# Masking the transposed probabilities instead of the right-hand side, and sending the last zero fill as one plain transfer

## The chip, the cores and the metric

The kernel runs on one core of a Trainium2 chip. The metric is the device time of one execution in microseconds (us); less is better. Engines are named as in the profile: PE (matrix multiplication), DVE (vector), ACT (scalar), POOL (GpSimd) and SP (sync). SP, ACT and POOL issue DMAs; 16 DMA engines carry them out.

## The reference, cut to what matters

One decode step of a transformer block, and the gradients of everything in it. The output is a row of 448 numbers; the caches have 8 heads of 32768 keys of 256 numbers, and only the last 4096 keys are attended to.

```
W = 4096
q = layernorm(x) @ wq;  k = k_cache[:, :, Sk - W:, :];  v = v_cache[:, :, Sk - W:, :]
p = softmax(q k / 16);  o = p v;  h = x + o @ wo
h2 = h + (gate(layernorm(h)) * up(layernorm(h))) @ w_down
outputs: h2, and d(x), d(k_cache), d(v_cache), d(wq), d(wo), d(w_gate), d(w_up), d(w_down)
```

All numbers are bf16. The gradients of the two caches have the full size of the caches, 134 MB each: zero for the first 28672 keys of each head, and for the last 4096 a sum of two outer products, since two query heads share a key head: dV = p dO and dK = dS q, one row per key.

## The kernel before, in words

**Zero fills.** The zero part of the cache gradients is written by DMA from a block of zeros in SBUF, `zeros`, 128 partitions by 8192 numbers (2 MB a transfer). The list `fills` has 103 such blocks (lines 119 to 126). POOL issues them: the first 55 at the start (lines 135 and 136), the next 47 from line 434 on, behind the second feed-forward block, and the last one, `fills[-1]`, at the end of the program in four pieces (lines 660 to 667). The pieces take their rows from 5, 3, 8 and 4 partitions: 10 rows of 576 B, 24 of 16384 B, 72 of 16304 B and 32 of 16384 B. Five more fills, `late_jobs`, four of 4 MB and one of 2 MB, are issued by SP (line 671).

**First pass** (lines 331 to 342): a loop over the 8 key heads computes scores and softmax, and moments of K and V. **Middle** (lines 363 to 493): the output projection, the feed-forward part and its backward pass.

**Second pass** (lines 605 to 655): a loop over the 8 key heads again, with its position `it` and its head `g`. For each head it

1. transposes V in blocks and multiplies (function `dots`, lines 245 to 262), which gives dP;
2. builds `pds`, 128 by 128: for each of 32 key tiles (4 quarters q of 8 tiles l) four columns, the probabilities and dS of two query heads, and transposes it on PE into `r_ps` (line 624), which DVE copies to SBUF as `rT` (line 626). Row 32 q + 4 l + i of `rT` has the numbers of key tile (q, l) and column i;
3. spreads dO and q of the head over 128 rows as `R_sb`, 128 by 512 (lines 627 to 633);
4. multiplies `R_sb` by the mask `tl_f`, 128 by 8, which is 1 where the row belongs to tile l: `RB_`, 128 by 8 by 512 (line 635), in one of two buffers `Rbig`;
5. for each l and q multiplies 32 rows of `rT` with 32 rows of `RB_[:, l]` on PE (line 643), which gives dV and dK of one key tile. Since the mask has zeros in 28 of the 32 rows, one tile comes out. DVE and ACT copy the results to SBUF (lines 647 to 651), in place of V and into one of two buffers at `dK_off`;
6. stores both, 2 MB each, by SP (line 653), and runs the jobs that `plan` gives to this position: the weight gradients (lines 541 to 599), which SP stores too.

Order of the work: a tile scheduler derives it from priorities and data dependences, so an edit may move instructions of any engine. SP's DMAs share eight semaphores in turn, and so do POOL's, so that each has at most eight DMAs in flight. In the program of SP the last entries are: the stores of the head at `it` 5, those of the feed-forward weights, the stores of `it` 6, one 4 MB late fill, the stores of `it` 7, and the three last late fills.

Of the kernel before, what the change touches and what calls it, by code (L numbers as in the profile page):

```python
# [7 lines left out]
bf16 = mybir.dt.bfloat16  # L8
f32 = mybir.dt.float32
AX = mybir.AxisListType.X  # L10
ALU = mybir.AluOpType
# [15 lines left out]
ZW = 8192  # L27
# [6 lines left out]
def kernel(  # L34
# [19 lines left out]
    def ar(off, n):  # L54
        return arena[:, off:off + n]
# [29 lines left out]
    VT_slot = [ar(RB + (40 + 2 * i) * KB, 2 * KB).rearrange("p (e t k) -> p e t k", t=4, e=2) for i in range(3)]  # L85
    Zr = ar(RB + 46 * KB, KB).rearrange("p (w k i) -> p w k i", w=4, k=32)
    rows2 = ar(RB + 47 * KB, 2 * KB)[0:16].bitcast(f32)
    Rbig = [ar(RB + 8 * KB * i, 8 * KB).rearrange("p (l n) -> p l n", l=8) for i in range(2)]
    dK_off = [RB + 16 * KB, A_off[2]]
    wst = [ar(A_off[3 + i], 16 * KB) for i in range(2)]  # L90
    dg_bc = ar(A_off[5], 2 * F).rearrange("p (i f) -> p i f", i=2)
# [36 lines left out]
    def send_fills(n0, n1, halves=False):  # L128
        for reg in fills[n0:n1]:
            if halves:  # L130
                ZQ.dma_start(out=reg.rearrange("p (k f) -> p k f", k=2), in_=zeros[:, 0:ZW // 2].unsqueeze(1).to_broadcast([128, 2, ZW // 2]))
            else:
                ZQ.dma_start(out=reg, in_=zeros)  # L133
# [229 lines left out]
    with tc.tile_pool(name="ps_mid", bufs=3, space=bass.MemoryType.PSUM) as ps_mid, \  # L363
# [34 lines left out]
        for n in range(len(BLOCKS)):  # L398
            f0, nb, w, wgu, wd = block_views(n)
            b0 = f0 // 128  # L400
            cs = slice(b0, b0 + nb)
            for b in range(nb):
                nc.vector.tensor_tensor_reduce(out=dgb[:, 0:D], in0=wd[:, b, :], in1=dh2_bc[:], scale=1.0, scalar=0.0,
                                               op0=ALU.mult, op1=ALU.add, accum_out=d_hh[:, b0 + b:b0 + b + 1])
            gu_ps = ps_mid.tile([128, 2, 5], f32, tag="mid", name="gu_ps")
            for i in range(2):
                for b in range(nb):
                    for k in range(4):
                        kp = DQ if k == 3 else 128
                        nc.tensor.matmul(gu_ps[:, i, b:b + 1], lhsT=wgu[0:kp, k, i, b::nb], rhs=X2_b[0:kp, k:k + 1], start=(k == 0), stop=(k == 3))  # L410
            nc.vector.tensor_copy(out=gu_f[:, :, cs], in_=gu_ps[:, :, 0:nb])
            for i in range(2):
                nc.vector.tensor_tensor(out=dgu_f[:, i, cs], in0=d_hh[:, cs], in1=gu_f[:, 1 - i, cs], op=ALU.mult)
            nc.vector.tensor_tensor(out=hh_f[:, cs], in0=gu_f[:, 0, cs], in1=gu_f[:, 1, cs], op=ALU.mult)
            nc.vector.tensor_copy(out=hh_bf[:, cs], in_=hh_f[:, cs])
            for i in range(2):
                nc.vector.tensor_tensor(out=diag[:, 0:w].rearrange("p (m b) -> p m b", b=nb), in0=ident_f[:].unsqueeze(2).to_broadcast([128, 128, nb]),
                                        in1=dgu_f[:, i, cs].unsqueeze(1).to_broadcast([128, 128, nb]), op=ALU.mult)
                for m in range(2):
                    bc_ps = ps_mid.tile([128, 320], f32, tag="mid", name="bc_ps")  # L420
                    nc.tensor.matmul(bc_ps[:, 0:w // 2], lhsT=ones_bf[:], rhs=diag[:, m * w // 2:(m + 1) * w // 2], start=True, stop=True)
                    nc.scalar.copy(out=dgb[:, w * i + m * w // 2:w * i + (m + 1) * w // 2], in_=bc_ps[:, 0:w // 2])
            for b in range(nb):
                nc.tensor.matmul(ffn_ps[:], lhsT=hh_bf[:, b0 + b:b0 + b + 1], rhs=wd[:, b, :], start=(b0 + b == 0), stop=(b0 + b == NF - 1))
            for c in range(4):
                kp = DQ if c == 3 else 128
                wc = wgu[0:kp, c].rearrange("p i f -> p (i f)")
                nc.vector.tensor_tensor_reduce(out=wc, in0=wc, in1=dgb[0:kp, 0:2 * w], scale=1.0, scalar=0.0,  # L428
                                               op0=ALU.mult, op1=ALU.add, accum_out=dhn[0:kp, c, n:n + 1])
            if n + 2 < len(BLOCKS):  # L430
                load_block(n + 2)
            if n == 1:
                nc.vector.memset(ar(ZW // 2, ZW // 2), 0.0)
                send_fills(HALF1, len(fills) - 1)

        dcat2 = workm.tile([128, 8], f32)
        nc.vector.reduce_sum(out=dcat2[:, 0:4], in_=dhn[:], axis=AX)
# [57 lines left out]
    with tc.tile_pool(name="work2", bufs=2) as work2, tc.tile_pool(name="lnw", bufs=1) as lnw, \  # L495
# [109 lines left out]
        for it, g in enumerate(order):  # L605
            V_sb = kv_at(V2_off[it])
            fill_vpad(it % 2, doT_bf[:, :, 2 * g:2 * g + 2])

            def evac(q, XT, ps):
                if q % 2:  # L610
                    nc.scalar.copy(out=XT, in_=ps)  # L611
                else:
                    nc.vector.tensor_copy(out=XT, in_=ps)  # L613
            dpT_ps = dots(V_sb, VT_slot, vpad[it % 2], rows2, ps_t, "tmp", evac)

            pds = work2.tile([128, 4, 8, 4], bf16, tag="pds")
            pv = pT_all[:, g].rearrange("p (q l) h -> p q l h", q=4)
            tmp = work2.tile([128, T, 2], f32, tag="tmp2")
            nc.vector.tensor_tensor(out=tmp[:], in0=dpT_ps[:].rearrange("p q l h -> p (q l) h"),
                                    in1=delta_bc[:, 2 * g:2 * g + 2].unsqueeze(1).to_broadcast([128, T, 2]), op=ALU.subtract)  # L620
            nc.vector.tensor_copy(out=pds[:, :, :, 0:2], in_=pv)
            nc.vector.tensor_tensor(out=pds[:, :, :, 2:4], in0=tmp[:].rearrange("p (q l) h -> p q l h", q=4), in1=pv, op=ALU.mult)
            r_ps = ps_t.tile([128, 128], bf16, tag="tmp")
            nc.tensor.transpose(r_ps[:], pds[:].rearrange("p q l i -> p (q l i)"), ident_bf[:])
            rT = work2.tile([128, 128], bf16, tag="rT")
            nc.vector.tensor_copy(out=rT[:], in_=r_ps[:])
            nc.vector.tensor_copy(out=Zr, in_=Z4[:, :, :, g, :].rearrange("p w e i -> p (w e) i").unsqueeze(2).to_broadcast([128, 4, 32, 4]))
            R_ps = ps_t.tile([128, 2, 2, 128], f32, tag="tmp")
            for w in range(2):
                for dh in range(2):  # L630
                    nc.tensor.matmul(R_ps[:, w, dh, :], lhsT=Zr[:, 2 * w + dh].rearrange("p k i -> p (k i)"), rhs=ident_bf[:], start=True, stop=True)
            R_sb = work2.tile([128, 512], bf16, tag="R", bufs=1)
            nc.scalar.copy(out=R_sb[:], in_=R_ps[:].rearrange("p w e n -> p (w e n)"))  # L633
            RB_ = Rbig[it % 2]
            nc.vector.tensor_tensor(out=RB_, in0=R_sb[:].unsqueeze(1).to_broadcast([128, 8, 512]),  # L635
                                    in1=tl_f[:].unsqueeze(2).to_broadcast([128, 8, 512]), op=ALU.mult)
            stV, stK = V_sb, kv_at(dK_off[it % 2])
            for l in range(8):
                for qp in range(2):
                    d_ps = ps_d.tile([128, 2, 2, Dh], f32, tag="d")  # L640
                    for qi in range(2):
                        q = 2 * qp + qi
                        nc.tensor.matmul(d_ps[:, qi].rearrange("p w d -> p (w d)"), lhsT=rT[32 * q:32 * (q + 1), :], rhs=RB_[32 * q:32 * (q + 1), l, :],  # L643
                                         start=True, stop=True)
                    t = 4 * l + 2 * qp
                    if qp:
                        nc.scalar.copy(out=stV[:, t:t + 2, :], in_=d_ps[:, :, 0, :])  # L647
                        nc.scalar.copy(out=stK[:, t:t + 2, :], in_=d_ps[:, :, 1, :])  # L648
                    else:
                        nc.vector.tensor_copy(out=stV[:, t:t + 2, :], in_=d_ps[:, :, 0, :])  # L650
                        nc.vector.tensor_copy(out=stK[:, t:t + 2, :], in_=d_ps[:, :, 1, :])  # L651
            for o_ap, st_ in ((out_3, stV), (out_2, stK)):
                LD.dma_start(out=o_ap[0, g, Sk - W:, :].rearrange("(p t) d -> p t d", t=T), in_=st_)
            for job in plan[it]:
                job()
            if it == 6:

                nc.vector.memset(ar(ZW, ZW), 0.0)

        flat = fills[-1].rearrange("p f -> (p f)")  # L660
        base = 0
        for p0, k, m, w in ((0, 5, 2, 288), (20, 3, 8, ZW), (64, 8, 9, ZW - 40), (0, 4, 8, ZW)):
            n = k * m * w
            ZQ.dma_start(out=flat[base:base + n].rearrange("(k m f) -> k m f", k=k, m=m),
                         in_=zeros[p0:p0 + 4 * k - 3:4, 0:w].unsqueeze(1).to_broadcast([k, m, w]))
            base += n
        assert base == 128 * ZW
        for o, g, n0, n1, f in late_jobs:
            reg = zero_rows(o, g, n0, n1, f)
            for i in range(reg.shape[0]):  # L670
# [30 lines left out]
```

## Time and profile before

| what | value |
|---|---|
| median of 4 runs | 797.76 us (796.17 to 797.96) |
| profiled execution, its own time | 797.22 us |
| its span, first to last instruction | 795.4 us |
| bytes moved by DMA | 334.77 MB |
| busy: PE, DVE, ACT, POOL | 59%, 55%, 25%, 8% of the span |

Times in the trace count from the start of the span. A group line gives the source line, engine, operation, operands with partitions x elements, the count, the busy time and the mean of one in ns, and the idle time ahead of it with what ended it. A window line gives for each engine the busy time and the number of instructions, then PE's granted clock, the share of the 16 DMA engines that was busy, and the rate.

### The profile page before, as it was taken

What the parts mean: (1) busy time and instruction counts of PE and PEld (TensorE: products, weight loads), DVE (VectorE), ACT (ScalarE), POOL (GpSimd) and SP (SyncE); (2) the same over time, 40 slices, a digit from 0 to 9 for tenths busy, and PEclk for the clock granted to TensorE, in tenths of its full rate; (3) what the DMA queues carried; (4) which work ended last, traced back from release to release, by engine and by line L of the source; (5) the groups of instructions that cost most, each with busy time, mean ns of one, the idle gap of its engine ahead of it and who ended that gap; (6) DMA issues with size and microseconds to landing.
All of it is one profiled execution on the core that took longest, in us unless ns stands there. A gap on an engine that the chain in (4) does not pass through costs nothing.

```text
span 795.4 us, 7324 instructions
## 1 busy us (share of the span) xinstructions
PE 470.7 (59%) x2926; PEld 220.4 (28%) x2926; DVE 436.7 (55%) x629; ACT 196.0 (25%) x309; POOL 63.4 (8%) x115
## 2 busy tenths in 40 slices
PE   0459999999999998251409477673450553722000
PEld 0333434344344433121208334330220210300000
DVE  2116584765846782263690679598653874964000
ACT  0142314134132201010102126362320441534000
POOL 4000000010101111100210001000000000010000
PEclk9989999999999999655558769695565556865555
DMA  9999999999999999999999999999999999999996
GB/s 350 430 429 429 431 429 431 430 428 426 431 423 425 429 418 414 422 422 425 431 429 424 421 430 427 427 428 427 423 424 424 423 425 422 428 419 417 430 438 297
DMA packets 29688, 334.77 MB, mean 421 GB/s; under 512 B 3150, under 2 KB 6230, under 8 KB 8150
## 3 DMA queue, kind: packets, MB, share of 16 engines
q0 software_dynamic: 16832, 216.01, 64.2%
q1 hardware_dynamic: 11382, 116.68, 34.9%
q10 hardware_dynamic: 1440, 1.61, 0.6%
q8 instruction: 23, 0.38, 0.2%
q14 instruction: 11, 0.09, 0.0%
HBM read 53.69 MB, written 280.59 MB: 420 GB/s over the span
## 4 chain that ended last, share of the span: by engine, by line
PE 39%; DMA 30%; DVE 15%; ACT 5%; issue 2%; another core or an unknown queue 0%; SPq 0%; DVEq 0%; ACTq 0%
DMA out_dram<-arena 21%; PE M_ps L317 13%; PE ok_ps L320 8%; PE rows_ps L256 6%; PE tr_ps L253 4%; DMA dh_bc<-in_grad_out_dram 4%; ACT arena L270 3%; DMA arena<-in_B_w_down_dram 3%; DVE arena L459 2%; PE dqb_ps L502 2%; DMA arena<-in_B_w_gate_dram 2%; DVE arena L635 2%; DVE arena L428 1%; DVE arena L514 1%; DVE arena L650 1%
## 5 line engine op out<-in xcount | busy, mean ns | idle before, releaser
L312 DVE TENSOR_TENSOR arena<-arena,p_f 128x2048 bf16<-128x2048 bf16 x64 | 145.4, 2286 | 60.5 <-PE M_ps L317 60.4
L317 PE MATMUL M_ps<-arena 128*128 128x512 bf16 x512 | 128.9, 380 | 0.2 <-ACT arena L323 0.2
L643 PE MATMUL d_ps<-arena,rT 32*128 32x512 bf16 x256 | 46.0, 506 | 116.4 <-DVE arena L651 67.4
L253 PE MATMUL tr_ps<-ident_bf,arena 128*128 128x128 bf16 x1024 | 89.4, 237 | 19.1 <-ACT arena L611 11.4
L256 PE MATMUL rows_ps<-arena,vpad 128*16 128x512 bf16 x256 | 87.2, 435 | 21.1 <-DVE arena L613 15.2
L133 POOL DMA_DIRECT2D out_dram<-arena x89 | 47.8, 539 | 528.5 <-DMA out_dram<-arena 494.0
L253 PEld LDWEIGHTS <-arena 128*128 128x128 bf16 x1024 | 66.9, 106 | 70.3 <-issue 61.8
L270 ACT COPY arena<-tr_ps 128x1024 bf16<-128x1024 bf16 x64 | 61.8, 1015 | 64.0 <-PE tr_ps L253 64.0
L647 ACT CAST arena<-d_ps 128x512 bf16<-128x512 f32 x64 | 37.7, 588 | 125.8 <-PE d_ps L643 125.8
L320 PE MATMUL ok_ps<-arena 128*16 128x512 bf16 x256 | 63.8, 381 | 0.9 <-DVE arena L297 0.9
L317 PEld LDWEIGHTS <-arena 128*128 128x128 bf16 x512 | 43.3, 99 | 59.0 <-issue 23.2
L611 ACT COPY arena<-tr_ps 128x1024 bf16<-128x1024 bf16 x32 | 32.6, 1019 | 94.3 <-PE rows_ps L256 34.6
L651 DVE CAST arena<-d_ps 128x512 bf16<-128x512 f32 x64 | 43.4, 678 | 13.6 <-DMA out_dram<-arena 13.6
L643 PEld LDWEIGHTS <-rT 32*128 32x128 bf16 x256 | 11.4, 95 | 142.0 <-issue 93.4
L650 DVE CAST arena<-d_ps 128x512 bf16<-128x512 f32 x64 | 43.7, 683 | 12.6 <-PE d_ps L643 12.0
L648 ACT CAST arena<-d_ps 128x512 bf16<-128x512 f32 x64 | 38.0, 594 | 14.4 <-DMA out_dram<-arena 14.4
L635 DVE TENSOR_TENSOR arena<-R_sb,tl_f 128x4096 bf16<-128x4096 bf16 x8 | 35.3, 4416 | 0.7 <-ACT R_sb L633 0.7
L256 PEld LDWEIGHTS <-vpad 128*16 128x16 bf16 x256 | 19.0, 91 | 58.1 <-issue 50.2
L320 PEld LDWEIGHTS <-arena 128*16 128x16 bf16 x256 | 19.1, 89 | 41.5 <-issue 20.3
L514 DVE CUSTOM_DVE_ANT_0 arena<-arena 128x4096 bf16<-128x4096 bf16 x3 | 13.1, 4420 | 24.5 <-ACT arena L507 24.5
L285 ACT ACTIVATE e_f<-cols_ps,nbias 128x32 f32<-128x32 f32 x16 | 4.5, 285 | 86.8 <-DVE nbias L281 86.8
L258 DVE COPY arena<-rows_ps 16x512 f32<-16x512 f32 x16 | 10.8, 676 | 26.4 <-PE rows_ps L256 26.3
(199 smaller groups left out, 389.1 us busy)
## 6 DMA issues: line engine op xcount, KB each, us to landing
out_dram<-arena POOLq DMA_DIRECT2D x102, 2048.0 KB, 52.3
out_dram<-arena SPq DMA_DIRECT2D x18, 2048.0 KB, 32.8
arena<-in_A_v_cache_dram SPq DMA_DIRECT2D x10, 2048.0 KB, 49.5
arena<-in_A_k_cache_dram SPq DMA_DIRECT2D x8, 2048.0 KB, 29.0
out_dram<-arena SPq DMA_DIRECT2D x4, 4096.0 KB, 43.1
arena<-in_A_wq_dram SPq DMA_DIRECT2D x2, 3072.0 KB, 20.6
arena<-in_A_wo_dram SPq DMA_DIRECT2D x2, 1792.0 KB, 14.2
out_dram<-arena SPq DMA_DIRECT2D x2, 1792.0 KB, 15.1
```

What stands on the lines that cost most here:

```text
L133: ZQ.dma_start(out=reg, in_=zeros)
L253: nc.tensor.transpose(tr_ps[:, dh, i, :], X_sb[:, 4 * q + i, dh * 128:(dh + 1) * 128], ident_bf[:])
L256: nc.tensor.matmul(rows_ps[:], lhsT=pad[:, dh, 16 * q:16 * q + 16], rhs=XT[:, dh].rearrange("p t k -> p (t k)"), start=(q == 0 and dh == 0 ...
L270: sT_ps = dots(kv_at(K_off[g]), KT_slot, vpad[g % 2], rows1, ps_c, "cols", lambda q, XT, ps: nc.scalar.copy(out=XT, in_=ps))
L312: nc.vector.tensor_tensor(out=pK, in0=K_sb[:, 4 * c:4 * c + 4, :].unsqueeze(2).to_broadcast([128, 4, 2, Dh]), in1=p_f[:, c::8, :].unsqueez ...
L317: nc.tensor.matmul(M_ps[:, vh, :], lhsT=V_sb[:, t, vh * 128:(vh + 1) * 128], rhs=pK[:, i, :, :].rearrange("p h d -> p (h d)"), start=(t == ...
L320: nc.tensor.matmul(ok_ps[:].rearrange("p k d -> p (k d)"), lhsT=ppad[g % 2][:, 8 * (t % 4) + t // 4, :], rhs=both(g, t), start=(g == 0 and ...
L635: nc.vector.tensor_tensor(out=RB_, in0=R_sb[:].unsqueeze(1).to_broadcast([128, 8, 512]), in1=tl_f[:].unsqueeze(2).to_broadcast([128, 8, 51 ...
L643: nc.tensor.matmul(d_ps[:, qi].rearrange("p w d -> p (w d)"), lhsT=rT[32 * q:32 * (q + 1), :], rhs=RB_[32 * q:32 * (q + 1), l, :], start=T ...
L648: nc.scalar.copy(out=stK[:, t:t + 2, :], in_=d_ps[:, :, 1, :])
L650: nc.vector.tensor_copy(out=stV[:, t:t + 2, :], in_=d_ps[:, :, 0, :])
L651: nc.vector.tensor_copy(out=stK[:, t:t + 2, :], in_=d_ps[:, :, 1, :])
```

## The change

The mask moves from the right-hand side (4096 columns) to the transposed probabilities (1024 columns): `rT` is not copied out of PSUM but multiplied by the mask on the way, once for each l, and the product on PE takes slice l of it with the unmasked `R_sb`. The buffers `Rbig` go; the two new operands have two buffers each. Independently of this, the last zero fill goes out as the others do, in one transfer of 128 rows behind the 102nd, and the four pieces go.

```diff
-    Rbig = [ar(RB + 8 * KB * i, 8 * KB).rearrange("p (l n) -> p l n", l=8) for i in range(2)]
+    rT_slot = [ar(RB + 2 * KB * i, 2 * KB).rearrange("p (l n) -> p l n", l=8) for i in range(2)]
+    R_slot = [ar(RB + (4 + i) * KB, KB) for i in range(2)]
...
-                send_fills(HALF1, len(fills) - 1)
+                send_fills(HALF1, len(fills))
...
-            rT = work2.tile([128, 128], bf16, tag="rT")
-            nc.vector.tensor_copy(out=rT[:], in_=r_ps[:])
+            rTm = rT_slot[it % 2]
+            nc.vector.tensor_tensor(out=rTm, in0=r_ps[:].unsqueeze(1).to_broadcast([128, 8, 128]),
+                                    in1=tl_f[:].unsqueeze(2).to_broadcast([128, 8, 128]), op=ALU.mult)
...
-            R_sb = work2.tile([128, 512], bf16, tag="R", bufs=1)
-            nc.scalar.copy(out=R_sb[:], in_=R_ps[:].rearrange("p w e n -> p (w e n)"))
-            RB_ = Rbig[it % 2]
-            nc.vector.tensor_tensor(out=RB_, in0=R_sb[:].unsqueeze(1).to_broadcast([128, 8, 512]),
-                                    in1=tl_f[:].unsqueeze(2).to_broadcast([128, 8, 512]), op=ALU.mult)
+            R_sb = R_slot[it % 2]
+            nc.scalar.copy(out=R_sb, in_=R_ps[:].rearrange("p w e n -> p (w e n)"))
...
-                        nc.tensor.matmul(d_ps[:, qi].rearrange("p w d -> p (w d)"), lhsT=rT[32 * q:32 * (q + 1), :], rhs=RB_[32 * q:32 * (q + 1), l, :],
+                        nc.tensor.matmul(d_ps[:, qi].rearrange("p w d -> p (w d)"), lhsT=rTm[32 * q:32 * (q + 1), l, :], rhs=R_sb[32 * q:32 * (q + 1), :],
...
-        flat = fills[-1].rearrange("p f -> (p f)")
-        base = 0
-        for p0, k, m, w in ((0, 5, 2, 288), (20, 3, 8, ZW), (64, 8, 9, ZW - 40), (0, 4, 8, ZW)):
-            n = k * m * w
-            ZQ.dma_start(out=flat[base:base + n].rearrange("(k m f) -> k m f", k=k, m=m),
-                         in_=zeros[p0:p0 + 4 * k - 3:4, 0:w].unsqueeze(1).to_broadcast([k, m, w]))
-            base += n
-        assert base == 128 * ZW
```

In the order of the instructions, the changed program has one more plain fill on POOL (103, without a wait on DVE), and on SP the 4 MB late fill that stood ahead of the stores of `it` 7 stands behind them; the 896-column store of the feed-forward weights stands between the stores of `it` 6 and `it` 7.

## The prediction

> **What bounds the kernel.** I read the 40 slices first, then the bytes, the windows at the end, SP's DMAs in order of time, and last the groups that the change touches.
>
> ```profile
> DMA  9999999999999999999999999999999999999996
> GB/s 350 430 429 429 431 429 431 430 428 426 431 423 425 429 418 414 422 422 425 431 429 424 421 430 427 427 428 427 423 424 424 423 425 422 428 419 417 430 438 297
> ...
> HBM read 53.69 MB, written 280.59 MB: 420 GB/s over the span
> ```
>
> From the first slice to the last but one the 16 DMA engines are 90% busy or more, at about 425 GB/s; 334.77 MB at that rate are 788 of the 795.4 us of the span. No other engine is over 59%. The chain of waits names PE and DVE for more than half, but only because a DMA queue with work left shows as no wait. So the end is set by the bytes, and by how evenly the 16 engines finish. The second shows in the windows at the end (PE, PEld, DVE, ACT, POOL busy; clock; DMA share; GB/s):
>
> ```profile
> 740.00:760.00 20.00, 0.00 (x0) 0.00 (x0) 0.00 (x0) 0.00 (x0) 0.00 (x0) 0.50 1.01 431
> ...
> 786.00:787.00 1.00, 0.00 (x0) 0.00 (x0) 0.00 (x0) 0.00 (x0) 0.00 (x0) 0.50 1.00 426
> 787.00:788.00 1.00, 0.00 (x0) 0.00 (x0) 0.00 (x0) 0.00 (x0) 0.00 (x0) 0.50 0.77 328
> 788.00:789.00 1.00, 0.00 (x0) 0.00 (x0) 0.00 (x0) 0.00 (x0) 0.00 (x0) 0.50 0.54 229
> 789.00:790.00 1.00, 0.00 (x0) 0.00 (x0) 0.00 (x0) 0.00 (x0) 0.00 (x0) 0.50 0.50 213
> 790.00:791.00 1.00, 0.00 (x0) 0.00 (x0) 0.00 (x0) 0.00 (x0) 0.00 (x0) 0.50 0.34 147
> 791.00:792.00 1.00, 0.00 (x0) 0.00 (x0) 0.00 (x0) 0.00 (x0) 0.00 (x0) 0.50 0.27 115
> 792.00:793.00 1.00, 0.00 (x0) 0.00 (x0) 0.00 (x0) 0.00 (x0) 0.00 (x0) 0.50 0.19 82
> 793.00:794.00 1.00, 0.00 (x0) 0.00 (x0) 0.00 (x0) 0.00 (x0) 0.00 (x0) 0.50 0.08 33
> ```
>
> No compute has run since 740. From 787 to 794 the engines fall out one by one. The shares add up to 2.69, which is 2.69 us of all 16 engines, spread over 7: had all ended together, that would have been some 4 us sooner.
>
> **Who ends when.** The trace keeps start, duration, size and queue of each DMA packet, not its engine. But an engine starts a packet 3 to 4 ns before its last one ends, so that the packets string into 16 chains, back from the end, where the starts lie apart. I did this from the end back to where the four pieces of the last fill run (about 735 to 749 on the packets' own clock, which is some 10.3 us ahead of the span's: the last packet ends at 804.4 on it). Every packet found a place. The chains fall into four kinds by what they hold of the fill: nine rows of 16304 B (8 chains); eight rows of 16384 B alone (3), or with a short row of 1152 B (4); and one chain with the short row only. Their ends:
>
> - 16304 B: 796.9, 797.2, 797.7, 798.0, 798.0, 799.9, 799.9, 800.2
> - 16384 B: 799.6, 800.2, 802.0, 802.9, 803.9, 804.1, 804.4
> - nothing but the short row: 801.6
>
> So the pieces give one engine next to nothing, and eight engines a little more than the other seven; the one that is spared still ends at 801.6, later than the mean of 800.4.
>
> **The change, part by part.**
>
> *The last fill.* It leaves the bytes as they are, and gives each engine eight rows of 16384 B. Rows of this size took 611 ns alone and about 618 while compute ran (means of the packets). The spared engine gains 8 x 0.618 = 4.9 us of work and loses its short row and about 30 packets of 4 B at 9 ns that belong to the pieces (0.3 us): 801.6 + 4.6 = 806.2. The eight lose one row (0.6 us), and everybody about 0.2 us of small packets. The last end moves from 804.4 to 806.2: **+1.8 us**. When the fill is issued doesn't matter: POOL's queue still moved the rows of the plain fills ahead of it when the pieces came, so it takes its turn in the same stream. POOL's wait goes, and nothing was behind it:
>
> ```profile
> POOL out_dram L664 <- DVE arena L651: 35.4, 1, 35.4
> ```
>
> *Rule against row.* The Trainium skill, "DMA: Bandwidth & Descriptors", section "Rules for kernel authors", asks for 128 partitions and at least 1 MiB per DMA, and its section on the anatomy of a DMA gives about 2.0 us fixed for each; by that, one transfer instead of four would save 6 us. The trace says that the fixed part is covered: the pieces take 32 to 35 us to land in a queue at a share of 1.01.
>
> *The mask.* The groups:
>
> ```profile
> L312 DVE TENSOR_TENSOR arena<-arena,p_f 128x2048 bf16<-128x2048 bf16 x64 | 145.4, 2286 | 60.5 <-PE M_ps L317 60.4
> L635 DVE TENSOR_TENSOR arena<-R_sb,tl_f 128x4096 bf16<-128x4096 bf16 x8 | 35.3, 4416 | 0.7 <-ACT R_sb L633 0.7
> L613 DVE COPY arena<-tr_ps 128x1024 bf16<-128x1024 bf16 x32 | 21.6, 680 | 3.0 <-PE tr_ps L253 2.4 <-PE rows_ps L256 0.3
> L626 DVE COPY rT<-r_ps 128x128 bf16<-128x128 bf16 x8 | 1.7, 213 | 0.0
> ```
>
> Eight of 4416 ns and eight copies of 213 go; eight products of 1024 columns out of PSUM come. From 2048 and 4096 columns the slope is 2130 / 2048 = 1.04 ns and the fixed part 156 ns, so 1221 ns for 1024. Bounds: 680 (a copy of that size out of PSUM) and 2286 (the 2048-column product). I take 1221, the same operation. DVE saves 8 x (4416 + 213 - 1221) = 27 us; by the bounds 19 to 32 us. PE's matmuls and weight loads keep count and shape (256 of each). The product waits for what the copy waited for, and holds the one PSUM buffer of its tag 1.0 us longer; the four R matmuls, which need that buffer next, wait for it, 8 us in all, but where they waited the big product came behind them: 33.6 us of PE waiting on line 635 go.
>
> None of the 27 us reaches the end. The second pass waits for its own stores: in the chain, DMA stretches of 15 to 43 us stand between the heads. SP's queue says the same (start, duration):
>
> ```profile
> 703.30 13.36 SPq L653 DMA_DIRECT2D out_dram<-arena  x2
> 716.72 11.36 SPq L671 DMA_DIRECT2D out_dram<-arena  x1
> 731.00 3.95 SPq L653 DMA_DIRECT2D out_dram<-arena  x2
> 736.96 4.75 SPq L671 DMA_DIRECT2D out_dram<-arena  x3
> ```
>
> Everything is issued by 742, and the engines work until 794. DVE time saved turns into waits for stores. Value taken: **0**. Its bounds: less compute beside DMA could make rows faster, 618 ns towards 611, over at most the last 30 us, 0.3 us; the other way, 0.
>
> *SP's order.* The 4 MB late fill moves behind the last stores. These may find SP's and POOL's queues empty; then the engines idle. At 731, 25.1 MB were left (the windows from there on), 14.7 MB of them in transfers issued at 731 or later; so 10.4 MB stood ahead, and 6.2 MB without that fill. At 425 GB/s that is 14.6 us of cover: the last head's compute may be 14 us later than now, and it has less to do. So 0. If the cover is gone, each us more costs one.
>
> **Sum.** 797.22 + 1.8 = 799.0 for an execution like the profiled one. The median of the runs is 0.54 above that execution, and I forecast the median: **799.5 us** (+0.2%).
>
> **Rivals.**
>
> 1. *The spared engine isn't always the slowest.* For it: it ended in the middle of the seven, and ends differ by 5 us among engines with equal bytes. If it comes out 2 us earlier, the 804.4 engine still ends last: 797.2 - 0.2 = 797.0, with the median's distance 797.5, no change.
> 2. *Faster: the ends even out.* Which engine is late may depend on the stream, and the pieces themselves may have made it uneven. If the spread falls to half, the last end comes 2 us sooner, and the median is 795.7; it decides once the engine that takes the 4.9 us is one of those that end before 799. Against it: the spared engine was late even though spared.
> 3. *Slower by more: a hole ahead of the last fills.* It needs the last head 14.6 us later than now. With 3 to 5 us of idle engines beyond the 1.8: 802.5 to 804.5. Against it: DVE has 27 us less to do.
> 4. *The mask pays after all*, if stores that come earlier shorten the stream: 796 at best. Against it: the engines have no gap to fill, and more than 50 us at the end pass without compute.
>
> **Chances.** Forecast 0.62, with its own range 798.5 to 801.5; rival 1 0.18; rivals 2 and 4 together 0.10; rival 3 0.10. A measurement of this kernel can tell about 0.2% from no change, 1.6 us: the border to slower is 799.4, inside the forecast's own range. I put three quarters of it, 0.48, above. So slower 0.48 + 0.10 = 0.58; same 0.14 + 0.18 = 0.32; faster 0.10. The range reaches from rival 1's 797.0 to 801.8, just past the forecast's own upper end.
>
> **What would show it.** Right: a DMA share of 1.0 up to about 787, then a longer tail in which the share falls to one engine (0.06) for the last 2 us; the chain that ended at 801.6 is last; a new DVE group of eight at about 1.2 us; DVE's busy time 27 us less, and DVE's and SP's waits for stores longer. Wrong: no lone engine at the end (rivals 1 and 2), or a share well under 1.0 between 730 and 760 (rival 3). Over 803 or under 796 would say that the engines' lags don't carry from one program to the next.

## The result and the profile after

The changed kernel takes **798.96 us** in the median (798.46 to 800.34, 38 runs); the kernel before, with more runs, 797.30 us (795.14 to 799.01, 56 runs). The ratio is 1.002, with a 95% interval of 1.0015 to 1.0025: slower by 1.66 us. The profiled execution after took 798.80 us, with a span of 797.0 us, 1.6 us more than before.

The page of the kernel after, DMA in 40 slices and in sums:

```profile
DMA  9999999999999999999999999999999999999995
GB/s 350 428 431 430 431 427 429 432 431 423 433 422 426 427 418 414 422 421 425 434 429 421 425 428 429 428 428 423 425 426 425 422 427 421 424 426 420 437 428 257
DMA packets 29352, 334.76 MB, mean 420 GB/s; under 512 B 2819, under 2 KB 5894, under 8 KB 7814
...
HBM read 53.69 MB, written 280.59 MB: 419 GB/s over the span
```

The same bytes move at nearly the same rates, slice by slice; only the last slice is emptier (257 GB/s instead of 297), because the DMA engines end less evenly. There are 336 packets fewer: 331 of them have 4 or 8 B, and the other five are the short rows of the pieces. The windows at the end show the tail (columns as before; the last two are the DMA share and GB/s):

```profile
740.00:760.00 20.00, 0.00 (x0) 0.00 (x0) 0.00 (x0) 0.00 (x0) 0.00 (x0) 0.50 1.02 432
...
789.00:790.00 1.00, 0.00 (x0) 0.00 (x0) 0.00 (x0) 0.00 (x0) 0.00 (x0) 0.50 0.35 147
790.00:791.00 1.00, 0.00 (x0) 0.00 (x0) 0.00 (x0) 0.00 (x0) 0.00 (x0) 0.50 0.12 49
791.00:792.00 1.00, 0.00 (x0) 0.00 (x0) 0.00 (x0) 0.00 (x0) 0.00 (x0) 0.50 0.19 82
792.00:793.00 1.00, 0.00 (x0) 0.00 (x0) 0.00 (x0) 0.00 (x0) 0.00 (x0) 0.50 0.11 49
793.00:794.00 1.00, 0.00 (x0) 0.00 (x0) 0.00 (x0) 0.00 (x0) 0.00 (x0) 0.50 0.08 33
794.00:795.00 1.00, 0.00 (x0) 0.00 (x0) 0.00 (x0) 0.00 (x0) 0.00 (x0) 0.50 0.08 33
```

Before, a third of the engines still worked at 790; after, only an eighth do, and yet the end is later. From 793 on the share is 0.08, about one engine of 16. The chains of packets, strung as in the prediction, say the same: 13 engines end from 797.0 to 800.6, and three behind them at 802.4, 804.3 and 806.2 (on the packets' clock).

The mask's groups, and SP's DMAs in order of time (start, duration):

```profile
L627 DVE TENSOR_TENSOR arena<-r_ps,tl_f 128x1024 bf16<-128x1024 bf16 x8 | 9.7, 1215 | 0.8 <-PE r_ps L625 0.8
```

```profile
705.95 5.68 SPq L652 DMA_DIRECT2D out_dram<-arena  x2
711.69 5.73 SPq L584 DMA_DIRECT2D out_dram<-arena  x1
731.20 1.63 SPq L652 DMA_DIRECT2D out_dram<-arena  x2
734.23 13.00 SPq L662 DMA_DIRECT2D out_dram<-arena  x4
```

DVE is busy for 410.2 us instead of 436.7. Its last stores are issued at 731.2; before, with 26 us more to do, at 731.0. Most of the time saved went into waits for stores that had not landed: those of DVE (all lines together) grew from 57 to 79 us. The longest, before and after (the columns: us in total, times, longest):

```profile
DVE arena L539 <- DMA out_dram<-arena: 22.4, 2, 15.6
```

```profile
DVE arena L540 <- DMA out_dram<-arena: 33.4, 3, 22.4
```

This is a job waiting for its buffer.

### The profile page after: what moved, and what is told of

Same layout as the page of the kernel before. It is cut to its first block, busy times and chain, and to the rows that moved or that the text cites. A ratio compares the mean times of both kernels' runs of the same rounds, so it can differ in the third digit from the quotient of the medians.

```text
span 797.0 us, 7310 instructions
## 1 busy us (share of the span) xinstructions
PE 470.6 (59%) x2926; PEld 220.1 (28%) x2926; DVE 410.2 (51%) x621; ACT 195.9 (25%) x309; POOL 61.1 (8%) x112
## 4 chain that ended last, share of the span: by engine, by line
PE 41%; DMA 27%; DVE 16%; ACT 4%; issue 2%; another core or an unknown queue 2%; SPq 0%; DVEq 0%; ACTq 0%
DMA out_dram<-arena 18%; PE M_ps L318 13%; PE ok_ps L321 8%; PE rows_ps L257 7%; PE tr_ps L254 5%; DMA dh_bc<-in_grad_out_dram 4%; ACT arena L271 3%; DMA arena<-in_B_w_down_dram 3%; DVE arena L460 2%; DVE arena L649 2%; PE dqb_ps L503 2%; DMA arena<-in_B_w_gate_dram 2%; DVE arena L545 2%; DVE arena L650 2%
## 5 line engine op out<-in xcount | busy, mean ns | idle before, releaser
L642 PE MATMUL d_ps<-arena 32*128 32x512 bf16 x256 | 45.1, 506 | 98.6 <-DVE arena L650 84.0
L642 PEld LDWEIGHTS <-arena 32*128 32x128 bf16 x256 | 10.9, 95 | 124.1 <-issue 77.4
L540 DVE TENSOR_SCALAR arena<-arena,xT 128x1792 bf16<-128x1792 bf16 (+1 forms) x9 | 7.7, 881 | 33.4 <-DMA out_dram<-arena 33.4
```

## The experiments

Theory: one DMA engine always has more to do than the others, the four pieces spared it, and the plain fill doesn't. Rival A: the mask, or the new order of SP's stores, made the kernel slower. Rival B: four pieces sent late are good in themselves, whichever engine they spare. The time of the kernel before that stands beside a run was taken on the same chip.

### One part of the change at a time

The mask edit with the four pieces kept:

```diff
-                send_fills(HALF1, len(fills))
+                send_fills(HALF1, len(fills) - 1)
...
+        for p0, k, m, w in ((0, 5, 2, 288), (20, 3, 8, ZW), (64, 8, 9, ZW - 40), (0, 4, 8, ZW)):
```

> The mask edit alone; the last fill stays in its four pieces. Theory (the end is set by the DMA engine that has most to move; the four pieces spare one that is always late): the last packet ends as before, no change against before, ratio 1.000 within 0.0007, 797.0 to 797.8 us, and DVE's busy time 27 us less than before. Rival A (the mask, or the order of SP's stores that it changes, made the kernel slower): ratio 1.002, about 799 us. Rival B (the pieces help only through their shape or their late issue): ratio 1.000 too.

Measured: 797.34 us against 797.37, ratio 0.9996 (0.9987 to 1.0004); DVE is busy for 410.4 us. The last packet ends at 804.3 on the packets' clock (804.4 before). In this program SP's late fill stands behind the last stores as it does after, and the kernel is no slower. Rival A is out.

The plain fill with the mask on 4096 columns:

```diff
-                send_fills(HALF1, len(fills) - 1)
+                send_fills(HALF1, len(fills))
...
-        for p0, k, m, w in ((0, 5, 2, 288), (20, 3, 8, ZW), (64, 8, 9, ZW - 40), (0, 4, 8, ZW)):
```

> The last fill alone goes plain; the mask stays on the 4096 columns. Theory: ratio to before 1.002, about 799.0 us, and a lone DMA engine (share 0.06 to 0.08) in the last 2 us. Rival A: ratio 1.000. Rival B: ratio 1.002 too.

Measured: 798.91 us, ratio 1.0019 (1.0011 to 1.0028). The last packet ends at 806.4, the one before it at 804.5. The windows 793 to 795 have the lone engine again:

```profile
793.00:794.00 1.00, 0.00 (x0) 0.00 (x0) 0.00 (x0) 0.00 (x0) 0.00 (x0) 0.50 0.12 49
794.00:795.00 1.00, 0.00 (x0) 0.00 (x0) 0.00 (x0) 0.00 (x0) 0.00 (x0) 0.50 0.08 33
```

The fill alone is the whole of the change's effect.

### How much cover DVE has

```diff
             nc.vector.tensor_tensor(out=RB_, in0=R_sb[:].unsqueeze(1).to_broadcast([128, 8, 512]),
                                     in1=tl_f[:].unsqueeze(2).to_broadcast([128, 8, 512]), op=ALU.mult)
+            nc.vector.tensor_tensor(out=RB_, in0=R_sb[:].unsqueeze(1).to_broadcast([128, 8, 512]),
+                                    in1=tl_f[:].unsqueeze(2).to_broadcast([128, 8, 512]), op=ALU.mult)
```

> The kernel before with the mask product on 4096 columns issued twice (the second writes the same again), which adds 35 us to DVE in the second pass. Theory (DVE's time in the second pass is covered by the stores): ratio 1.000 within 0.001, about 797.3 us. Rival A (the second pass bounds the end, and the mask's cost was hidden in the changed kernel by something else): up to 35 us more, ratio 1.01 to 1.04.

Measured: 797.37 us against 797.33, ratio 1.000 (0.9989 to 1.0011). SP's last entries and the windows of this kernel:

```profile
763.39 2.42 SPq L655 DMA_DIRECT2D out_dram<-arena  x2
765.87 2.83 SPq L673 DMA_DIRECT2D out_dram<-arena  x2
```

```profile
740.00:760.00 20.00, 3.69 (x25) 0.66 (x26) 15.68 (x14) 6.44 (x12) 1.12 (x2) 0.50 1.00 420
760.00:780.00 20.00, 1.23 (x8) 0.21 (x8) 2.58 (x4) 2.15 (x4) 0.00 (x0) 0.50 0.99 420
```

The last stores go out 32 us later than before, compute runs until after 760, and the DMA share is still 1.0: the queues held enough. The order of SP's entries moved as well: three 4 MB late fills (issued at 690, 721 and 738) stand ahead of the last stores here, two before and one after the change. So neither 27 us less nor 35 us more of DVE in the second pass is seen at the end.

### Shape and time of the pieces, or their weights

The last fill in four pieces again, sent last, but each of 128 rows of 4096 B, the same for all engines:

```diff
-                send_fills(HALF1, len(fills))
+                send_fills(HALF1, len(fills) - 1)
...
+        for i in range(4):
+            ZQ.dma_start(out=fills[-1][:, i * 2048:(i + 1) * 2048], in_=zeros[:, 0:2048])
```

> The changed kernel with the last fill sent last and in four pieces, but with equal bytes for all 16 engines (128 rows of 4096 B each). Theory (weights decide, not shape or time of issue): as the changed kernel, ratio 1.002, about 799 us. Rival B (four pieces sent late help by themselves): ratio 1.000.

Measured: 798.92 us against 797.12, ratio 1.0025 (1.0016 to 1.0034). Last packets at 804.3 and 806.3, as with the plain fill. Rival B is out: four late pieces without weights bring nothing.

### Sparing another engine

A first attempt moved the pieces on by eight engines, with a piece of 13 partitions:

```diff
+        for p0, k, m, w in ((0, 13, 1, 288), (52, 3, 8, ZW), (0, 8, 9, ZW - 52), (64, 4, 8, ZW)):
```

> The changed kernel with the last fill in four pieces again, turned on by eight engines: 13, 3, 8 and 4 partitions instead of 5, 3, 8 and 4, so that another engine is spared and the one spared before gets nine rows. Theory: that engine's end is 801.6 - 0.4 + 9 x 0.616 = 806.7 on the packets' clock, 2.3 us behind the last end of before: ratio 1.003, 799 to 800 us. Rival B (any engine will do; what helps is four pieces sent late): ratio 1.000, 797.3 us.

Measured: 812.59 us, ratio 1.0177 (1.0156 to 1.0198), far more than any theory expected. In the packets, the 72 rows of 16280 B took 941 ns in the mean and up to 1413, and some of 16384 B up to 2544; before, rows of the pieces took 620 to 625 ns in the mean, 665 at most. It looked as if a plain fill gave each engine eight certain partitions, the pieces of before kept to them, and mine didn't. The next two kernels separate this from the question asked. One spares an engine of the other half and keeps every row of the pieces that counts on the partitions of a plain fill:

```diff
+        for p0, k, m, w in ((0, 8, 9, 8056), (64, 4, 8, ZW), (80, 4, 2, 288), (0, 8, 2, 288), (64, 5, 2, 288), (84, 3, 8, ZW)):
```

> As the run that spared another engine, but each engine reads the partitions that it reads in a plain fill: 8 engines (that of the old spared one among them) nine rows of 16112 B, 4 and 3 engines eight rows, one engine of the second half only short rows. Theory (one engine is always late and it is the one that the four pieces spare): its end is 801.6 - 0.4 + 9 x 0.61 = 806.7 on the packets' clock, ratio 1.003, 799 to 800 us. Rival B (any engine will do): ratio 1.000. Rows take 0.61 to 0.64 us, not 1.1 to 2.5.

Measured: 799.74 us against 797.12, ratio 1.0034 (1.0021 to 1.0046). The rows of 16112 B took 616 ns in the mean. The last packet ends at 807.2, on a chain read as one with nine rows of 16112 B, 2.4 us behind the next chain; 806.7 was expected. The fill is as uneven as before, only for the wrong engine, and its median is 0.8 us above that of the changed kernel, though the intervals overlap. Rival B is out.

The other keeps the weights of before and moves every row by four partitions:

```diff
+        for p0, k, m, w in ((4, 5, 2, 288), (24, 3, 8, ZW), (68, 8, 9, ZW - 40), (4, 4, 8, ZW)):
```

> The four pieces with the weights of the kernel before, all rows read from the partitions four further on, so that each engine reads what its neighbour reads in a plain fill. If the long rows of the run that spared another engine (1.1 to 2.5 us) come from reading another engine's partitions: rows of 1.1 us or more in the pieces, and ratio 1.005 to 1.02. If they came from the 13-partition piece or from the engine that was spared: rows of 0.61 to 0.64 us and ratio 1.000.

Measured: 804.42 us, ratio 1.0094 (1.0079 to 1.0109). Rows of 16304 B took 746 ns in the mean and up to 1302. The window in which they run shows something that a reader should know (before, then this run; DMA share and GB/s last):

```profile
720.00:740.00 20.00, 3.31 (x24) 0.55 (x20) 7.72 (x12) 6.44 (x12) 0.00 (x0) 0.50 1.02 415
```

```profile
720.00:740.00 20.00, 2.46 (x16) 0.44 (x16) 5.83 (x10) 4.79 (x10) 0.00 (x0) 0.50 1.00 357
```

All engines are "busy", and some rows take twice as long: a share of 1.0 means that packets are under way, not that they go at full speed. Against the four pieces of before, this run changes the partitions that are read (and the mask, which alone changed nothing), so the partitions make the slow rows here, with a ratio inside the range expected. That they also explain the run with the 13-partition piece is likely, not shown: what happened there row by row isn't settled.

### A better balance

The eight early engines get more, the seven less, the spared one next to nothing:

```diff
-        for p0, k, m, w in ((0, 5, 2, 288), (20, 3, 8, ZW), (64, 8, 9, ZW - 40), (0, 4, 8, ZW)):
+        for p0, k, m, w in ((0, 5, 2, 332), (20, 3, 4, ZW), (64, 8, 13, 7845), (0, 4, 4, ZW)):
```

> The changed kernel with the last fill in four pieces with stronger weights: none to the same spared engine, four rows of 16384 B to seven engines, thirteen of 15690 B to eight. Theory, from the chains of before: the eight end at 799.0 to 802.3, the seven at 797.1 to 801.9, the spared one at 801.6; the last end is 802.3 instead of 804.4, ratio 0.9974, about 795.2 us. Rival B: ratio 1.000. If which engine is late changes from run to run: between 0.999 and 1.002.

Measured: **795.56 us** against 797.37, ratio 0.9977 (0.9968 to 0.9986), which beats both kernels. The last packet ends at 803.1 (802.3 expected). The windows:

```profile
788.00:789.00 1.00, 0.00 (x0) 0.00 (x0) 0.00 (x0) 0.00 (x0) 0.00 (x0) 0.50 0.76 328
789.00:790.00 1.00, 0.00 (x0) 0.00 (x0) 0.00 (x0) 0.00 (x0) 0.00 (x0) 0.50 0.61 262
790.00:791.00 1.00, 0.00 (x0) 0.00 (x0) 0.00 (x0) 0.00 (x0) 0.00 (x0) 0.50 0.20 82
791.00:792.00 1.00, 0.00 (x0) 0.00 (x0) 0.00 (x0) 0.00 (x0) 0.00 (x0) 0.50 0.08 33
```

More engines work at 789, and the share is 0.00 from 792 on: the tail is steeper.

To see which of three engines was late there, I split their piece in three, each of 17 rows:

```diff
-        ..., (20, 3, 4, ZW), ...
+        ..., (20, 1, 17, 1927), (24, 1, 17, 1926), (28, 1, 17, 1925), ...
```

> The stronger weights again, with the piece for three engines split into one piece for each of them, 17 rows of 3854, 3852 and 3850 B, so that the chains of packets tell the three apart. Theory: time as with the stronger weights, ratio 0.9975 to 0.998, and two of the three end last, some 3 us behind the four engines with the same bytes.

Measured: 807.75 us against 797.12, ratio 1.0136 (1.0123 to 1.015). The pieces left as eight rows of 7708, 7704 or 7700 B and one of about half that, not as 17, and the rows of 15664 B behind them took 820 ns in the mean and up to 1307, as if the engines no longer met their own partitions. How a piece of one partition moves on to the next engine isn't known from these runs, so the three were not told apart. The run is inconclusive on its question.

Finer weights without that:

```diff
-        for p0, k, m, w in ((0, 5, 2, 332), (20, 3, 4, ZW), (64, 8, 13, 7845), (0, 4, 4, ZW)):
+        for p0, k, m, w in ((0, 5, 2, 348), (20, 3, 2, ZW), (64, 8, 13, 8001), (0, 4, 5, ZW)):
```

> As the stronger weights, with two rows of 16384 B for the three engines of which two ended last there, five for the four engines that ended early, thirteen of 16002 B for the eight, none for the spared one. Theory: the last of the three comes 2 x 0.62 = 1.2 us sooner, 803.1 to 801.9, and the spared one ends at 801.7; the eight 0.2 us later, up to 801.7. So ratio about 0.996, 794.3 us. If which engine is late changes from run to run, no better than with the stronger weights: 0.9977.

Measured: 795.59 us against 797.33, ratio 0.9984 (0.9973 to 0.9994), no better than the coarser weights. The last four chains end at 802.0 to 802.8, where 801.9 was to be the last. So the ends were foretold to about 1 us only, which is as much as there was to gain. No gain is also what the expectation names for the case that which engine is late changes from run to run; on the scale of 1 us this run doesn't exclude that.

## Why the prediction was right, point by point

- **What bounds the kernel**: right, and shown. 26 us less or 35 us more of DVE changed nothing; 2 MB dealt out differently among the engines changed the time by -1.8 to +2.6 us with rows of about 16 KB that took 593 to 625 ns in the mean.
- **The last fill, +1.8 us**: the last packet was to end at 806.2 and ended at 806.2; the engine behind which it hid, at 804.4 less 0.2, ended at 804.3. The hit to 0.1 us is partly luck: the packets' clock is 10.46 us ahead of the span's before (not 10.3) and 10.75 after, so that on the span's clock the last packet moved from 793.94 to 795.49, by 1.55 us, about as the time did (1.6 for the profiled executions, 1.7 for the medians). That the last chain is the engine spared before isn't marked in the packets, and the chains are less sure than the prediction says: of the 2399 packets from 735 on, 231 have more than one packet that starts 3 to 4 ns before their end, so the ends of the chains are clear, but not which chain held which rows. The identity follows from sums instead. In the plain fill only the spared engine gets more than before. In the run that spared another engine, an engine with nine rows in place of eight gains 0.6 us and would end at 805.0 at the latest; only the one spared before, with nine rows in place of none, can reach the 807.2 that was measured (806.7 was worked out).
- **From the profiled execution to the median, +0.54 us**: the term that was mis-sized. It came from four runs of before; over 56 runs their median is 797.30, as good as the profiled 797.22. Without it the forecast is 799.0, and 798.96 was measured.
- **The mask, 27 us of DVE, nothing at the end**: right. The operation took 1215 ns (1221 expected), DVE's busy time fell by 26.5 us. The 8 us of waiting for the R matmuls did not come: 1.2 us, since in six of the eight heads PE had 11 to 18 other instructions to run between the transpose and these matmuls.
- **SP's order, 0**: right: the mask edit alone brings the same order, and its time is that of before. The 14.6 us of cover were not measured: in the run with two products the last stores go out 32 us later at no cost, but that program had three 4 MB late fills ahead of them and the changed one has one, so the two figures are not for the same queue.
- **The rule on large transfers**: four pieces cost nothing by their number. With equal weights they took as long as one (ratios 1.0025 and 1.002 to before, intervals overlapping).
- **Rivals**: 1 (the spared engine isn't always the slowest) fell with three programs that end at 806.2 to 806.4; 2 and 4 (faster) and 3 (a hole) have nothing in the windows: the share is 1.02 from 720 to 760. A slip in the chances changes nothing here: three quarters of 0.62 are 0.47, not 0.48.

Open: why some engines have more to do with the same bytes. It isn't slower rows at the end: the last eight rows of 16384 B of the chains that end at 804.3 and 806.2 took 611 ns each, those of the chain that ends first, at 797.0, 611 to 618. So the lag is older than these rows; where it comes from wasn't tried.

## What to carry to other kernels

Where the DMA engines are busy from end to end, look at how the share falls in the last microseconds: its area is what evening out can bring (here 4 us), and work taken off other engines brings nothing. A transfer dealt out unevenly on purpose is worth something only for the engine that is really late, so find which it is by sparing another, and keep every engine on the partitions it reads in a plain transfer. A distance between one execution and a median of four is noise, not a term of the sum.

## What the runs showed of the hardware that I had not expected

- Rows of the four pieces read four partitions further on took up to 1302 ns (16304 B, mean 746) instead of 625, and slowed the kernel by 0.94%. The Trainium skill, "DMA: Bandwidth & Descriptors", section "The descriptor swizzle", says that in a transfer that writes 128 partitions each engine has a certain set of eight partitions, all on one port. Here partitions are read; the runs fit the same sets (616 ns on them, 746 off them), and show what it costs to leave them. No run here shows the ports.
- The DMA share was 1.00 at 357 GB/s in one kernel and 1.02 at 415 GB/s in another, in the same window.
- With equal bytes the two last ends keep their places: the last two chains end at 804.3 and 806.2, 804.5 and 806.4, 804.3 and 806.3 in three programs (the changed one, the plain fill alone, the four equal pieces). The third from the end comes at 802.4, 803.1 and 802.1.
